# DeltaNet and SwiGLU on one core: eighteen sums of weight words from GpSimd to VectorE, other useless products at the start, and a new order of issue

## The chip, the cores and the metric

The kernel runs on one core of one Trainium2 chip. The metric is the device time of one execution in microseconds. Its engines run beside each other, each its own queue in order: TensorE (PE, with its weight loads PEld), VectorE (DVE), ScalarE (ACT), GpSimd (POOL), and SyncE (SP), which issues nearly all DMAs.

## The reference

Four batches, eight heads, 768 steps and heads of 48 go through the DeltaNet recurrence. The result, as 3072 tokens of 384 values, goes through an RMS norm and a SwiGLU feed-forward of width 1536. All of it is float32.

```python
k_n = k / (np.linalg.norm(k, axis=-1, keepdims=True) + 1e-06)
for t in range(S):
    y[:, :, t] = einsum('bhd,bhde->bhe', q[:, :, t], state)
    v_old = einsum('bhde,bhd->bhe', state, k_n[:, :, t])
    state = state + beta_t * einsum('bhd,bhe->bhde', k_n[:, :, t], v[:, :, t] - v_old)
x  = y.transpose(0, 2, 1, 3).reshape(B * S, H * D)          # 3072 x 384
xn = x / sqrt(mean(x * x, -1) + 1e-06) * rms_g
g  = xn @ w_gate                                           # 384 x 1536
out = (silu(g) * (xn @ w_val)) @ w_out                     # 1536 x 384
```

## The kernel before

**Chunks.** The 768 steps are cut into 12 chunks of 64. Within a chunk the recurrence is a triangular system, which is solved by an inverse; only the 48x48 states pass from one chunk to the next. Chunks 0 and 1 have their inverse made on VectorE by blocks of 16, in one long chain (L711 to L873: scaled scores, a transpose, small eliminations in 128x8 to 128x256 pieces, then products with the off-diagonal blocks on TensorE at L833 and L866). From chunk 2 on the chunk's matrices are shuffled by DMA and solved in another form (L935 to L1016).

**One chunk's recurrence.** K is loaded and squared (L604, ScalarE), summed over a head (L605, VectorE) and raised to a power for its norm (L609 and L628, GpSimd); K and Q are turned by TensorE (L560) and copied out (L570, L572); the scores are K times K (L692) and Q times K (L583). V is scaled by beta (L1145), multiplied with the inverse (L1202), with K's part (L1226; its operand comes from L833 by the copies L842 and L844), each copied out to `u` (L1216, L1218, L1238, L1240, L1245, L1247), and with the masked scores `pt` (L650) into the output (L1180). The products with the state stand at L1103, the state's update at L1273, its copy out at L1399. Then come the sums of squares (L1298, L1316), the root on GpSimd (L1323), the scaling (L1334, L1338), a turn (L1361), and the feed-forward.

**Feed-forward.** For chunks 0 and 1 it is the plain one: the up products for gate and value (L1433), the gating (L1441 on ScalarE, L1442 on VectorE), the down products (L1415). From chunk 2 on the products are saved in part by sums of weight blocks, made once on VectorE (L1491, L1493) and used at L1528 and L1585.

**Weights.** `weights()` brings the three weight matrices in as 18 pieces. The words of a piece are split by ScalarE into a high part (L500) and a low part (L501), the high part is shifted by three bits on VectorE (L495), and the sum of the two (L498) is written to `w_in` or `wo_sb`, from where TensorE reads it. A piece is 128 x 768 words; the buffers `xf`, `kk`, `more` and `tmp` hold the parts.

**What sets the order.** Each operation is recorded by `P.add(engine, duration, function, priority, ...)` and nothing is issued at that time. `Plan.run` issues all of them in the order that the string `ORDER` gives: two characters for the number of one operation, so that an operation added or taken away shifts the numbers of those behind it. The order is thus written out for every engine and queue, SyncE's DMAs too. The durations in `P.add` serve only to place useless products: where the plan leaves TensorE idle for more than 0.8 us, before `UNTIL` = 110 us of the plan, a list of them is put in front of the next TensorE operation. Such a product multiplies the identity with itself (L1707; widths of 128, 256 or 512 columns) into a bank that is not in use. A zero in the list stands for a tiny product of 32x1 (L1705). The first list, at time 0, is written by hand:

```python
    if a == 0.0:
        return [4, 4] + [0] * 13
```

One product in float32 is two records or more in the trace: the list's two products of 512 columns are four records, its thirteen tiny ones 26.

Of the kernel before, what the change touches and what calls it, by code (L numbers as in the profile page):

```python
# [12 lines left out]
ALU = mybir.AluOpType  # L13
# [3 lines left out]
C = 64  # L17
W = 32
# [26 lines left out]
    ",=*S*R,>,?,r+g(k,@,A*T,B+j*U,C,s,D(p*V,E,t,F(q,G(r,H,I*W(v,u*^(x(s*O*X.X*Y(u*_(t*`*Z(w*|,J.Y*[.Z*d*a,v,K*f*M*e*b*~,L"
    "*g.[*j,M+$*k*h*c*],N*t+%+k,O*l*i.]+#*u*p*N+h,P*v*P+(*w,Q*}+,,R+&*m.^,S*q+l*n+',T+-*x*o,W+)+.+m._+**y*r+4,U+/*z,X+2*s"
    "+n,V+5*{+6+p,x/F+3+:+7+++8.`+o,c+0+>+q,e+9,b.a+;,^+s+?+r,f,y):,[.c,d.b+B,g.n,'.g+F+C+<.d+@.e+t+=+x,(,`+u+N+G.f+A,a+H"
    "+1+v/E+J+D+y,h+w+K,_+z+{.5,Z+I,i+L,]+E,Y+|,j+O,{.h+P+M.i,l+},n,z,k,m.6.o.7+T+~+Q+V/M,#.;,$+U/L,%,&.8+W&.,~.j-$/G.k-&"
    ".l.m.p+R.q/H.r.s.t.<.u+Z.v+S/I.9.w-'.x/J+X+[.y-%&/.=+].z.:-#-(.{.>.|/K+Y-*1/.?-).@+_.W-+10.}11-0+`+^.~.B,|-,.A-1+b-2"
    "+a.C--12-8/#-..D-6.E-3.F/$-N-7-4-/-:-9/%-<13-5/&-P-=.G-R-Q/'-;-F.V-S->14-G-V/(.H-H/),}-B-I-Z-O-C/*-T15-[-D/+-J-?.I-U"  # L50
    "-c-E/,-W-]-d//-K-@-a/.-L16/-0h1y-M-A17-b-^.J0j-g-_18-X-e19-h-i/N-f/=1D-q/:-`-j1<-m-r1:-}1;-s-n-k1=-Y/<-o-l-t/2-p-u/9"
    "-y/8.#0i/1-v/;.K1>-w1?/>-x.L-{/3/O-z/7/?.M.)/4.N/@1E/6.O.'/R.P.Q/C/P/A/5-~/B/0-|.R.S.%.T.(/D.*1x/Q1@.-.$1A1B.&1C1F1G"
    "0n1H..1I1J.01K0k/T0o1L.U.+1M1z1N1O/V1{/U/X1|1P/W0l/Z.,/Y1}1Q0p.10m1R1S/].2/[1T.40q2$1~1U/_/^3b/c0r0s/e/`0t3c/d0%0u./"
    "/f/S0v/i1V.30'1W0x0w/k1X3e/j/m0y/g1Y/a3d/o1Z/n/l1[0)/b1]/p/u3f/h1./y1^0(2#/v0*/q0z/z/}1b/{/|012%0&3g0-/w1_020+1a/r1`"
    "2&/s0,/x091-3h0.030{/~0:2)070#040/1k0?0$1h2(081p0;/t3w4N3i0=1c0<0|053>1o061l0@3j1g2'0A1m0>0C1n3k3@1f3l0G0}0D3o1q0E0H"
    "3p0K001r3n0F3x3m0B0S3?0I4O0J1e0L1i1s0~1j0M0U1d0N1t3r0Q1v1#0O3q1$1w0[2+1%0Y0T1u1&0P0V0R3D1'1(1)1*3A0]0W1+3B1,3F3s0Z3C"
# [12 lines left out]
    ";U;X;Y9i8>;Z9d;[;]8?<1;^;_<2;`9k;a<39m;b9l8@;&8C;c9j8B9g9n;d9e9o;e8D8A;#8E9q<48F9p=t9u9r9w9v9{;f=u<6:7;%=v;g9}9x;'9~"
    ";h9|=w9y9h;i:%<5;(:#;):&;*:';j:$=x:/;+9z;k9s:+;,:0:9:,:1:;;-:(:::2:3=y:)9t:8;l:?:-;.;m:<:=;/:.;n:C:*;o:>:f=z:4;p9f:D"  # L70
    ";@:E:@;0;t:K:F;q:I={:G:5:A:M:L:6;1<7=|:J;r:N;s:H:O:B=};?=~:U:P;2:Q:b>$:V>#:Y<%:R:W>&:^:X:S;y:Z=P>%:T:[<=:_<8:];3:`:c"
    ">-<$:h:a:d:g=Q>(:e<:<#:l;v;4;u>':n;5;};6:j>.;{:i:o<&;7:m;w;8;~;9:r;::k<><9;z;;=R;<:p;x;=;><;:s>);|>*:t>+<?>,>/<A>0>1"
    ">2>3<'>4=S<(>5<B>6<)>7<C<-:q<*>8<G<,=T>9<@:v<+<D>:>;=V:w><:y<E<<=X=W=U:u<K>=:x=Y<F<H>><I<Q<L<M<R=r<S<N<W<J<T=Z<O=[<U"
    "<X=^<j>?=]<b<V>@=_<^<c=`<Y>A<d=a<l<P=b<e<Z<k<n<_<m<p>B<o<`=s<r<[<a<q<f=c<s<v>a>C<x<g<w<h<|<y=d<~<i>D<}=$<]=#<z=&<t=%"
    "=(=e>E='=,>c>F=0=-=<<u=.=)=f<{>G=*=/>J=1=4=8>I=2>d>H=3=g>b?x=+=h=5=i?{=j=9===6=>?|=7=k>S=:>f>W=l=B=m>V=n>O=;=?>P=o=D"
    ">U=@=C>X=E>R>N=p>K=q=H=A>g=I=K>Y>M=F>T>Z>h>L=J>Q>i=G?y>k>j>[>l>m>`?}=L>^>n>_>]?z>s=M=N>o>t=O>u>e>p?~>q>{@$@#>v>y@%>z"
    ">w>|?#@&?5?$?7@'>r@(>}?->~@)?9?.@*?)?/?:?0?%?*?6?A@+?&@,?;>x@-?'?8?(?1?+?<?=?,?B?C?2?>?I?3@.?D?G?4?J?K?H?M?L@/?S?N?O"
    "?T?W?P@0?[?Q?X?E?d?R?Y?]?U???Z?^?V?@@1?f?F?e?_?b?`?a?j?c?l@2?h?m@3@4?k?g@5?p@6?i@7@8@9@:@;?n@<?q?s?r@=?o@?@>?t@@@A@C"
    "@B?u@E@D?v@I?w@F@h@J@O@K@P@Q@L@U@R@M@j@G@V@S@N@`@T@k@l@a@p@H@b@m@c@[@i@t@]@n@u@d@o@W@q@e@v@X@f@|@Y@w@z@g@x@Z@^@y@~@_"
    "@{A$A#@}A*A%A&A+A.A,A'A2A-A(A/@rA:A)A0A1A3@sA<A4A;A5A6A7A?A8A=A9ALADAKA>ABAAAFACAEA@AMAGAHAJAIANAPAO"  # L80
# [176 lines left out]
def kernel(  # L257
# [17 lines left out]
    nc = tc.nc  # L275

    B, H, S, D = q.shape
# [17 lines left out]
    ident = sbt("ident", [128, 128])  # L295
# [98 lines left out]
    P = Plan()  # L394
# [72 lines left out]
    def weights(first, last):  # L467
# [14 lines left out]
        for n, (dst, src, keys) in list(enumerate(todo))[first:last]:  # L482
# [14 lines left out]
            def added(dst=dst.bitcast(U32), top=tiled(top), rest=tiled(rest)):  # L497
                nc.gpsimd.tensor_tensor(out=dst, in0=top, in1=rest, op=ALU.add)  # L498
# [5 lines left out]
            P.add("POOL", 1.87, added, pr, r=cvk + cak, w=done)  # L504
# [131 lines left out]
    qkeys = [("q2", 0, 0), ("q2", 0, 1), "q2p"]  # L636

# [239 lines left out]
    def prep(c):  # L877
# [824 lines left out]
    def filler(n, warm):  # L1702
        for w_ in n:
            if not w_:
                nc.tensor.matmul(warm[0:32, 0:1], ident[:, 0:32], ident[:, 0:1])  # L1705
                continue
            nc.tensor.matmul(  # L1707
                warm[:, 0 : 128 * w_].rearrange("p (w n) -> p w n", n=128), ident, ident[:, None, :].to_broadcast([128, w_, 128])
            )
# [33 lines left out]
```

## Time and profile before

| | us |
|---|---|
| runs | 660.82, 663.33, 663.36 |
| median | 663.33 |
| profiled execution | 663.93 |
| its span in the trace | 662.2 |
| TensorE busy | 650.7 (98%) |
| VectorE busy | 538.9 (81%) |
| ScalarE busy | 300.1 (45%) |
| GpSimd busy | 172.1 (26%) |

The profile comes from one execution, which is not one of the three timed runs. Times in the timeline count from the span's start. In rows of the timeline the first number is the start and the second the duration, then follow the engine, the line, the operation with its output and input and its shape; in brackets stands how long the engine idled before it and who ended that. In rows that group instructions the total and the mean in ns stand behind the bar. In rows by stretch each engine's busy time stands with its count of instructions in brackets, then TensorE's granted clock (1.00 is full), the share of the DMA engines and GB/s.

### The profile page before, as it was taken

To read this page: it belongs to the slowest core of one execution; us is meant where nothing else is said; L and a number is where in the kernel's file an instruction comes from. 1 tells how busy PE (TensorE), PEld (TensorE's weight loads), DVE (VectorE), ACT (ScalarE), POOL (GpSimd) and SP (SyncE) were. 2 spreads that over 40 slices of the span, in tenths; PEclk is the share of its full clock that TensorE was granted. 3 is DMA by queue.
4 is the path that set the end of the run, shared out by engine and by line. 5 is a ranking of instruction groups with operands and counts; after the bars stand their busy time and mean duration, and the time that the engine had idled before them with its cause. 6 is when DMAs were issued, how large, how long until landed. Compare 5 with 4: busy or idle time off the path is not lost.

```text
span 662.2 us, 23310 instructions
## 1 busy us (share of the span) xinstructions
PE 650.7 (98%) x9976; PEld 597.9 (90%) x9976; DVE 538.9 (81%) x1125; ACT 300.1 (45%) x712; POOL 172.1 (26%) x219
## 2 busy tenths in 40 slices
PE   9999999999999999899999999999999999999997
PEld 5587777877799999899999999999999999999997
DVE  5969779999799788898898898898899888457363
ACT  4776653235247245345344445444444354243240
POOL 4364790131600610520511330520511300000000
PEclk9998999999999999999999999999999999999999
DMA  9897754736295577276356476566167324211101
GB/s 221 224 229 190 245 138 89 122 54 103 75 135 99 129 146 117 35 151 111 71 103 120 90 142 102 87 128 95 41 122 122 71 49 82 37 38 25 25 2 24
DMA packets 270583, 69.36 MB, mean 105 GB/s; under 512 B 257488, under 2 KB 262736, under 8 KB 270160
## 3 DMA queue, kind: packets, MB, share of 16 engines
q1 hardware_dynamic: 269360, 67.63, 51.4%
q8 instruction: 78, 1.28, 0.8%
q10 hardware_dynamic: 1120, 0.25, 0.2%
q14 instruction: 25, 0.20, 0.1%
HBM read 49.76 MB, written 22.02 MB: 108 GB/s over the span
## 4 chain that ended last, share of the span: by engine, by line
PE 92%; DVE 4%; ACT 2%; issue 1%; POOL 0%; DVEq 0%; POOLq 0%; ACTq 0%
PE bank L1528 41%; PE bank L1585 20%; PE bank L1433 8%; PE bank L1415 5%; PE bank L1103 3%; PE bank L583 3%; PE bank L1707 2%; PE bank L1180 2%; PE bank L1166 2%; PE bank L1273 1%; PE bank L560 1%; PE bank L1045 1%; PE bank L1065 1%; PE bank L833 1%; PE bank L866 0%
## 5 line engine op out<-in xcount | busy, mean ns | idle before, releaser
L1528 PE MATMUL bank<-xf,w_in 128*128 128x128 f32 x1440 | 180.5, 276 | 0.0
L1528 PEld LDWEIGHTS bank<-xf,w_in 128*128 128x128 f32 x1440 | 170.2, 192 | 2.1 <-DVE acc L990 0.2
L1538 DVE TENSOR_TENSOR tmp<-tmp,bank 128x512 f32<-128x512 f32 x180 | 120.0, 682 | 42.1 <-PE bank L1528 36.4
L1528 PE MATMUL bank<-xf,more 128*128 128x128 f32 x960 | 122.0, 276 | 0.0
L1528 PEld LDWEIGHTS bank<-xf,more 128*128 128x128 f32 x960 | 114.6, 192 | 0.8
L1540 ACT COPY tmp<-bank 128x512 f32<-128x512 f32 x120 | 68.1, 586 | 95.9 <-PE bank L1528 69.5
L1544 ACT ACTIVATE tmp<-tmp 128x256 f32<-128x256 f32 x120 | 47.6, 415 | 72.3 <-DVE tmp L1538 72.1
L996 DVE TENSOR_REDUCE acc<-acc 128x30 f32<-128x90 f32 (+4 forms) x150 | 70.9, 473 | 5.2
L1585 PE MATMUL bank<-wo_sb,hf 128*128 128x192 f32 x360 | 64.0, 329 | 0.0
L935 POOL TENSOR_TENSOR at<-at,beta_b 128x256 f32<-128x256 f32 (+3 forms) x32 | 22.0, 718 | 158.1 <-DMA at<-dkk 139.1
L990 DVE TENSOR_TENSOR acc<-acc,at 128x60 f32<-128x60 f32 (+4 forms) x150 | 53.0, 353 | 10.5 <-POOL at L970 7.4
L1585 PEld LDWEIGHTS bank<-wo_sb,hf 128*128 128x128 f32 x360 | 58.1, 190 | 1.2 <-issue 0.4
L1545 DVE TENSOR_TENSOR hf<-tmp 128x256 f32<-128x256 f32 x120 | 47.6, 416 | 4.8 <-ACT tmp L1544 3.9
L628 POOL TENSOR_TENSOR knrm<-ksum,half 128x16 f32<-128x16 f32 x11 | 32.8, 2982 | 41.8 <-DVE ksum L607 40.2
L1415 PE MATMUL bank<-wo_sb,hf 128*128 128x384 f32 x96 | 35.6, 504 | 0.6 <-issue 0.6
L1433 PE MATMUL bank<-xp,w_in 128*128 128x256 f32 x144 | 35.2, 390 | 0.9 <-DVE hf L1442 0.9
L1016 POOL COPY acc<-acc 128x128 f32<-128x128 f32 x40 | 17.1, 459 | 69.1 <-DVE acc L996 67.7
L1433 PE MATMUL bank<-xf,w_in 128*128 128x256 f32 x144 | 33.1, 383 | 0.0
L1433 PEld LDWEIGHTS bank<-xp,w_in 128*128 128x128 f32 x144 | 27.0, 192 | 6.3 <-DVE hf L1442 1.3
L1385 DVE TENSOR_TENSOR xf<-xf 128x256 f32<-128x256 f32 (+1 forms) x70 | 29.1, 446 | 2.3 <-ACT xf L1355 1.8
L1433 PEld LDWEIGHTS bank<-xf,w_in 128*128 128x128 f32 x144 | 26.9, 190 | 4.3
L1322 POOL TENSOR_SCALAR ms<-ms 128x2 f32<-128x2 f32 x11 | 3.6, 331 | 93.6 <-ACT bank L1310 93.6
(221 smaller groups left out, 1024.5 us busy)
## 6 DMA issues: line engine op xcount, KB each, us to landing
at<-dkk SPq DMA_DIRECT2D x20, 256.0 KB, 4.3
vt<-in_v_dram SPq DMA_DIRECT2D x24, 192.0 KB, 4.3
k<-in_k_dram SPq DMA_DIRECT2D x23, 192.0 KB, 4.3
out_dram<-tmp SPq DMA_DIRECT2D x46, 96.0 KB, 2.2
dks<-k SPq DMA_DIRECT2D x14, 256.0 KB, 2.8
kt<-dks SPq DMA_DIRECT2D x28, 128.0 KB, 3.2
more<-in_moe_w_gate_dram SPq DMA_DIRECT2D x4, 768.0 KB, 7.0
more<-in_moe_w_out_dram SPq DMA_DIRECT2D x4, 768.0 KB
```

Source lines behind the costliest of these rows:

```text
L628: P.add("POOL", 2.95, lambda: nc.gpsimd.tensor_tensor(out=knrm[i2], in0=ksum[i2], in1=half, op=ALU.pow), pn, r=[("ksum", i2), "half"], w=[ ...
L990: nc.vector.tensor_tensor(out=acc[:, 1:3, 0:n, j + 2 : W].rearrange("p a i t -> p i a t"), in0=acc[:, old, 0:n, j : j + 2, None].to_broadc ...
L996: nc.vector.tensor_reduce(out=acc[:, new, 0:n, j + 2 : W], in_=acc[:, lo : lo + 3, 0:n, j + 2 : W].rearrange("p a i t -> p i t a"), axis=A ...
L1385: P.add("DVE", V(128 * n), lambda dst=dst, a=a, b_=b_, op=op: nc.vector.tensor_tensor(out=dst, in0=a, in1=b_, op=op), pxv, r=[("xp", 0), ( ...
L1415: nc.tensor.matmul(po[p].t[:, 0:DM], hf[:, spot(f), 128 * p : 128 * p + 128], wo_sb[:, spot(f)], start=(f == f0), stop=(f == f1 - 1), skip ...
L1433: nc.tensor.matmul(ps.t[:, TOK * side : TOK * side + TOK], w_in[:, side, h_, 3 * t + i_, n : n + 128], x_[:, 2 * t : 2 * t + 2].rearrange( ...
L1528: nc.tensor.matmul(g.t[:, 128 * z : 128 * z + 128], fac[:, side, 128 * f : 128 * f + 128], xf[:, xs], start=(begin and z == 0), stop=False ...
L1538: P.add("DVE", V(512), lambda t=t, g=g: nc.vector.tensor_tensor(out=t, in0=t, in1=g.t, op=ALU.add), -1, r=[g], w=[tk], last=g)
L1540: P.add("ACT", A(512), lambda t=t, g=g: nc.scalar.copy(t, g.t), -1, r=[g], w=[tk], last=g)
L1544: P.add("ACT", A(256), lambda t=t: nc.scalar.activation(out=t[:, 0:256], in_=t[:, 0:256], func=ACTF.Silu), -1, w=[tk])
L1545: P.add("DVE", V(256), lambda t=t, f0=f0, p=p: nc.vector.tensor_tensor(out=hf[:, spot(f0) : spot(f0) + 2, 128 * p : 128 * p + 128], in0=t[ ...
L1585: nc.tensor.matmul(g.t[:, 0:192], a_[:, f], b_[:, f], start=(begin and f == 0), stop=(f == 5), skip_group_check=True)
```

## The change

1. In `weights()` the sum of the high and low words (L498) is issued on VectorE instead of GpSimd. In the built program that is one instruction over half words, 1536 in each partition, for most pieces written as 3 rows of 512; the other operands and the order of the four steps of a piece are as before.
2. The first list of useless products becomes two of 512 columns and one of 256 columns, in the place of two of 512 and thirteen of 32x1.
3. A new function `ahead` records twelve of the tiny products as an operation of the plan, recorded in `prep()` for chunk 0 ahead of the turn of Q. In the built order they stand behind the 64 records of the scores and the turn of the betas (L660).
4. `ORDER` is another string: all operations of all engines and queues have a new order, and the places and widths of the later useless products follow from it. In sum the useless products have 10,624 columns for 11,520. In the built program VectorE has 8 of the 18 sums ahead of the last small elimination of chunk 1 (L762 before), three of them between chunk 1's scaled scores and that step; the other ten stand ahead of the first step on chunk 2's matrices (L935 before). In TensorE's order fifteen up products follow the state's update of chunk 0 where twelve did, and the state's product L1103 comes ahead of chunk 1's L583 and no longer behind it.

Lines from L638 on are 9 or 10 higher in the changed kernel (L1145 is L1155, L1433 is L1443).

```diff
@@ ORDER = ( ... )   every line of the string is replaced
@@ def fillers(a, b):
     if a == 0.0:
-        return [4, 4] + [0] * 13
+        return [4, 4, 2]
@@ weights()
             def added(dst=dst.bitcast(U32), top=tiled(top), rest=tiled(rest)):
-                nc.gpsimd.tensor_tensor(out=dst, in0=top, in1=rest, op=ALU.add)
+                nc.vector.tensor_tensor(out=dst, in0=top, in1=rest, op=ALU.add)
...
-            P.add("POOL", 1.87, added, pr, r=cvk + cak, w=done)
+            P.add("DVE", 0.97, added, pr, r=cvk + cak, w=done)
@@ ahead of qpart()
+    def ahead(n, pr):
+
+        def tiny():
+            for _ in range(n):
+                nc.tensor.matmul(banks[0][0:32, 0:1], ident[:, 0:32], ident[:, 0:1])
+
+        P.add("PE", 0.07 * n, tiny, pr, r=["ident"], size=4 * n)
+        P.ops[-1].ready = 10.0
@@ prep()
         if c == 0:
+            ahead(12, 14.0)
             P.urgent = 300.0
             qpart(0)
@@ def filler(n, warm):
         for w_ in n:
-            if not w_:
-                nc.tensor.matmul(warm[0:32, 0:1], ident[:, 0:32], ident[:, 0:1])
-                continue
             nc.tensor.matmul(
```

More of the change, by code (lines that the diff above doesn't have):

```diff
@@ new lines @@
+    "#|#g#~#}#h#r#1$##t#2$$#?$l#E$%$&#]$)$($'$*$>$+#J%L$-$,#D$/$.#N#K$0#L#@%O$3#O$q$4#P%z$5$?#F$@#Q$m$7$A$6%M$B#G&$$n$o#="
+    "%P$C#;#i%N#l#j$r#9#A$E#k$D$G$F$h$H$b$t$I$v$p$J$K$j%Q#8$T$L#B$M$U%y$i$V$O$W$N$1%$%[$X$Y$P%U$Z$Q$S$8$[$]$R$^%R%V&7$9${"
+    "%W%S$k$d&C&8%T$s%X$c$_%)$u&9&;%Y%Z&:$e&<%](%$f&?%{#6&=%^$a&>&@%_%`$2$`%a$w&E%|'$$}%b$x&&%c&A%3&F'%%%&%%}%d#5&D&G&B%~"
+    "'&&'%f&I&(%&&H$|%'&J%e%h%8$~&K%#%=%.%g%5%(&{&L&)$y%+%k&M&#%*&~&N'B%l%m%j%B%9&O%4%,%i'C&S&|%-'E$z%:%n%;%>&T&}%p%/%o%<"
+    "'F%s%@%?&U%u'Q'?&*%q%6(&%t&X%r'#'D%0%A%v%G%1#7&P%2%w%x'G&Q%C&R'''H'I&Y&V'K&W('%7'J&Z'L'+%D'M&_#:((&[%H#<()&`'(')'*&]"
@@ new lines @@
+    "%J(*','N&a%I&+'<'R'-&b&d'.'@(z'0({&e'/'A%E(+'1'O&i%K'>'2)_&j&f&g&,&1'4%F(-&k&n'3&2'=(,)b'P*B&^'S)`&c'T'U)a&5)c'V'8&3"
+    "'W&o'9'5'X':'6';)d'7'Y'Z)<)f'[)e&h&p)i'])j&m&l&4'^&6&r)h'_)g&s&q'`(6'a'b(:'c(;'d'e(7(.'f)l)k&t)+(8(<'g(9(=(/)>&x)8)?"
+    "'j'h(>(|'k&u'i(}(?),)-(D(@(0(~(E's(1'u)='r(B(C(A(F'v)#)n'q)m(I'y)o'x't(G)@(J'n)p'l'p(N)q)r(K'w)s'm'z'o)t*A(O)u'{*H(L"
+    ")v'|&z(P(S(2)w($*I(#'})x'~(H&y(4)y)B)z(M(Q){(3*C(X)|)A)D(Y)C*D(T*E)})~)E*F(U(Z*#*$(R(V*%,q)$(^*&(5([*G&w)](c*')F)G(_"
+    ",*)H*(**(d*)).)^*+,-)/,+,p)9(W,,(`,.)0+d*7(e(a)I*0)%,/*5)&)J*1(h)'*9,0(f*3,1)1*4(i)L+f,4,<*J*8(m)K*,)2,3):,5(n,2*2)3"
@@ new lines @@
+    ")Q*.)M+e*6)R(])4)N*/)O)S)((j*-)P*:)T)5,7*K)6,6*;,=,x)U)V*<)W&-*L(b*?)X(o(k*=,w)Y*@+g)7*>)Z*P))+j)**N(g)[+k,8&v(p,r*M"
+    ",9*R,:+h,;,>(l*S,?,s,@,A,B*T,C(q,D*U,t,E&.,F(r,u,G*V,H(s,I,J*X(w*W(t*Z+i,v(u*Y*_.Y(v*[(x*a*`*e,K.Z(y*},L*f.[+#*b*g,M"
+    "*c*k.],N*h*]*i+l*d*l+$*m*^*j,O*u*n*q.^*v*Q+%,P*w+m,Q+&*x*r*~+),R*s._,S+'/G+n,T*t*O+-+o*o+(,U*y+.+/+*.`*z+5,X+0*{,V+3"
+    "*p+6,W*|,y+q+7,Y+4+;/F+8.a+1+9+p+++?+r+:,b.b,),f+<+t,e+s,z+@,c+=.c,g+,);+G.d,h+A.f+C+>.e+H+y.g+D+u+z+O.h+2+v+w,],(+x"
+    "+E,d,{+{+I,_+B+|.6,[+}+F+~,|,i.j+Q+J,Z+M,j,a.7+P.o,`,#+K,^.p,k.i+L-#+U,$,l+W,},o,m.8,n&/,%.9+N+X.<,&.:+R,'+S.k.l-$.m"
@@ new lines @@
+    "/H.n.q,~-%.r+T.s.;/N.t-'.u+V/I.>.v+[.=.w/J.x.y/K.?.z.{+]+Y.|-&+_&0.}+^-+/L.W10-)+Z.@.A+`-*.~-(11.B12/#--1z+a.C-,+c-1"
+    "+b.D-.-3-213.E-7.X.F/M/$-9-8.G/%-/-O-:/&-=14-4-Q/'-5-;->-S-0-<.H/(-G-T-6-?15-H-C/)-I-R.I-J-[/*-P-D-W/+-@-U-E16-]/,-K"
+    "-V-d-X/--L-Y-^//-F-M.J-Z-b17/00i/.-N-_1y-c18/O-e-f-A/91:-B.K19-h/:-g1=-j-`-i/1-n-a/8-z/=/P-k/>-o1>-l-r1E1<-{1;/Q-v1F"
+    "/<-s/4-~-w/5-t-p/S-m-x-u/;-q.L/?1?.$1@-y.M0j/7.N-|.#/6.O.*/2/@.(/3.P/T0k.Q-}.R.S.&2$.T.).U.+.%1A/A/R1B..1C/D1D/E1G/C"
+    "/B1H.'1I1J0o1K1L0l1M0q0p1N.,1{1O0m.V./0n1P.1/W.01|/U0r1}/X1Q1R1~/Y.-1S.2/Z1T/V1U/[.32#.5/^0s/].43c1//`/_0&0t1V3d0v/d"
@@ new lines @@
+    "3e0u/a/f4O/e0w/j1W/l/g/k3f1X0x0(2%/b/m1Y0*0y/c0z/p1Z0+/n1[3g/q/r/o1]/h/z2&1^/v0{/i/{1_020)3h/|2'/}1b/w0.0'0|/s/x1`0,"
+    "031./~/y3i0-0:0/1c0#041a0;00080$1l051m0@0%1i093j0}0</t061o0>/u1k010=1f2)3k1q0A1p0?3?1e3l2(1n3m0D0~3@0B073n0H0E3o3p1r"
+    "0F0I3q0L0P4P0J1s0C0T3x1d0M1h1#0N0O1t1$3r0G1%0K3B1&1j1v1g1'1w1(1u0V3s1)1x3A3y1*0R0U1+0Q4W0Z0S0]2*4V1,3E1-0[0^0X0W3t3F"
+    "3u4Q3v3w3z0a3{0Y3|3}3~4R4#2.4$0b4S0d4%202/4&4T224'210_4(4)244*264U0`2X69230e254+6:0c272:6;0f4,0h2@0g2;2<4-6<2B2A4.2,"
+    "2F2C2=2Z2G2>3C2D4/6=2P402E3G2-2H2?282Q2]412R3D2L2I2[293H6>2S2^422+2Y432_443I2M2a453J2N2`2T6?3L3K2O2e462b3M482U2g492f"
@@ new lines @@
+    "2V2k3N2h3O2m6@2J3P2o472W2K7&6A2l4X2n4>2p2q4B6B2w6C3Q2r6D2s2x6N6G2{6E2t2i6F2c3#3a6O4C2j2|4Y3R2y2u3$4F2}3+4E2~3%2d4G2v"
+    "6I2z3'3S3-3(3,6H3&3)4D3*3b314[4Z333T3/4=347'3.4@6J4H4<306K5r4_6L3U4I6M326P4;4J6Q4A5t3V6R354?5s6S6T4N4:4K6U3W3X6V4L7."
+    "3Y4M373Z6W6X366Y5x3[3]5u3^6Z3;7(383_5z3`6[4a7)3<5v3=4c7*5y4b4`6]5w4e3:4d7+4]6^5{4f6_4g6`4m4h4^4i7,5|9X8l5}5/3>4n5~39"
+    "4o4j6#6a8m4u6$7-4p4s9Y6b516c4t4w6%6d8o4v4y6&6e4x536'4z4k4q8n4{6f4l6g5'684r54678p5#6h525(5;6(5$5)575*6k7/506j5+5%4|55"
+    "8q5,4}6l705<6)5&568H6i715=588r5C5>5A4~5?8I6*5-5D5E5.596s5B5I5:6v5F5@6r5G8s6x6z5M5H6y6p8t5N6+5J6n5Q8v5Y6w8u6u5U729%5R"
```

66 lines of the change are left out of this document (18 added, 48 removed).

## The prediction

> **What bounds the kernel now.** I read the page's shares and its chain first, then the windows by stage, the useless products by themselves, the chain of waits over the first 60 us, and last the timeline and the groups around the edited steps.
>
> ```profile
> PE 650.7 (98%) x9976; PEld 597.9 (90%) x9976; DVE 538.9 (81%) x1125; ACT 300.1 (45%) x712; POOL 172.1 (26%) x219
> PE 92%; DVE 4%; ACT 2%; issue 1%; POOL 0%; DVEq 0%; POOLq 0%; ACTq 0%
> ```
> ```profile
> 60.00:100.00 40.00, 39.08 (x696) 30.21 (x696) 29.89 (x56) 25.39 (x49) 31.24 (x21) 0.99 0.72 200
> 100.00:662.00 562.00, 555.85 (x8337) 526.98 (x8335) 464.35 (x958) 234.77 (x574) 112.13 (x172) 1.00 0.47 86
> ```
> ```profile
> 0.00:44.20 44.20, 23.74 (x68) 12.30 (x68) 1.00 0.92 211
> 44.20:60.00 15.80, 0.18 (x1) 0.00 (x0) 0.92 0.72 223
> ```
>
> The columns of the windows are the stretch, the busy time of PE, weight load, VectorE, ScalarE and GpSimd, then the granted clock. TensorE is busy 98% and 92% of the last chain is its own. But the last two rows, which hold the useless products alone, show that 23.74 us of its busy time before 44.20 us is filler. So the program has two halves. From about 60 us TensorE has a full queue (39.08 of 40, then 555.85 of 562 us, and a few per cent of records can be missing), and its work there is the same in both kernels: nothing can be gained, only lost. Before 60 us TensorE waits for VectorE and ScalarE, and the gain or loss of this change is made there.
>
> ```profile
> 1.41 3.78 PE bank L1707 x4
> 5.19 1.48 PE bank L1705 x26
> 6.67 1.90 PE bank L560 x8
> ```
> ```profile
> 5.79 0.84 ACT L604 ACTIVATE r<-k 128x768 f32<-128x768 f32 x1 [2.50 <-DMA k<-in_k_dram]
> ```
>
> **The start.** ScalarE begins on K at 5.79 us, when the load has landed. TensorE turns K only at 6.67, because the thirteen tiny products are still running (1.48 us). In their place stands one product half as wide as those before: two of the four records at 3.78/4 = 0.95 us, halved, are 0.95 us. So K's turn starts at 5.19 + 0.95 = 6.14, **0.5 us earlier**, and the steps behind it that have only this to wait for move with it. The twelve tiny products come back behind the scores and the betas' turn, at 1.48 x 12/13 = 1.4 us at the same speed, or less at the full clock; they delay q's turns by that, and a filler follows those in the new order too. That filler is the cover, since ScalarE copies q's turns only behind two sets of scaled scores: I charge nothing, and 1.4 us at most if the copies come up against them.
>
> **The sums.** Eighteen sums leave GpSimd and join VectorE's in-order queue.
>
> ```profile
> L498 POOL TENSOR_TENSOR w_in<-xf,tmp x6: 1812/1827/2017, 27.5 to 82.7; 128x768 uint32<-128x768 uint32 x6
> ```
> ```profile
> L495 DVE TENSOR_SCALAR xf<-xf 128x768 uint32<-128x768 uint32 x9 | 8.2, 909 | 1.2 <-ACT xf L500 1.0
> L495 DVE TENSOR_SCALAR kk<-kk 128x768 uint32<-128x768 uint32 x4 | 2.2, 553 | 1.2 <-ACT kk L500 1.2
> L1493 DVE TENSOR_TENSOR more<-more,w_in 128x512 f32<-128x512 f32 x1 | 0.7, 691 | 0.0
> L935 DVE TENSOR_TENSOR at<-at,beta_b 128x1024 f32<-128x1024 f32 x1 | 1.2, 1217 | 0.0
> ```
> ```profile
> 28.83 1.12 DVE L495 TENSOR_SCALAR xf<-xf 128x768 uint32<-128x768 uint32 x1
> 29.68 1.95 POOL L498 TENSOR_TENSOR w_in<-more 128x768 uint32<-128x768 uint32 x1
> 29.88 2.56 DVE L1145 TENSOR_TENSOR vt<-vt,rb 128x768 f32<-128x768 f32 x1
> 45.61 0.61 DVE L711 SCALAR_TENSOR_TENSOR acc<-m1bd,side,acc 128x128 f32<-128x128 f32 x2 [1.32 <-ACT acc L706]
> 47.67 2.17 DVE L711 SCALAR_TENSOR_TENSOR acc<-m1bd,side,acc 128x128 f32<-128x128 f32 x2
> 91.85 2.30 DVE L1493 TENSOR_TENSOR more<-w_in 128x512 f32<-128x512 f32 x1
> ```
>
> The trace has no such sum on VectorE. Two floating-point rows of the same form give a slope: (1.217 - 0.691)/512 = 1.03 ns an element, so 768 words at one word a cycle are 0.69 + 256 x 1.03 = **0.95 us**. The new program holds the sum as 1536 half words; one half word a cycle would be 1.217 + 512 x 1.03 = **1.74 us**, the other end. I take 0.95, because the shift of the same words (0.553 us for 768) runs no slower than a word a cycle. Eighteen are 17.1 us (31.3 at the other end).
>
> [...]
>
> VectorE gets something back. While GpSimd adds, VectorE's own work is stretched: V's scaling takes 2.56 us and ends 0.8 us after the sum beside it; by the slope it needs 0.95. The surplus is 1.61 there, (0.909 - 0.553) x 9 = 3.2 in the shifts of xf, 2.17 - 0.61 = 1.56 at the second pair of L711, and 2.30 - 0.69 = 1.61 at the last row against the undisturbed form of its line: together **8.0 us**. Net VectorE takes on 17.1 - 8.0 = 9.1 us, 23.3 at the other end. GpSimd loses 18 x 1.83 = 33 us, worth nothing by itself (0% of the chain).
>
> ```profile
> 24.12 1.48 POOL L885 TENSOR_TENSOR k<-k,krec 128x768 f32<-128x768 f32 x1 [7.13 <-DVE krec L632]
> 52.65 3.04 POOL L628 TENSOR_TENSOR knrm<-ksum,half 128x16 f32<-128x16 f32 x1 [2.53 <-DVE ksum L607]
> 53.07 0.29 DVE L754 TENSOR_TENSOR at<-at 128x128 f32<-128x128 f32 x1
> ```
>
> GpSimd keeps K's scaling (1.48) and the power steps. A power step stretches nothing: the two-input step of VectorE inside it takes 0.29 us for 128 elements. K's scaling has no such neighbour in the trace; if it held up a sum for its whole length three times, that were 4.4 us of VectorE's time, and I leave it in the range of the rival that fills VectorE.
>
> [...]
>
> **What becomes of it before 44 us.**
>
> ```profile
> 26.24 0.90 ACT L501 ACTIVATE tmp<-more 128x768 uint32<-128x768 uint32 x1
> 26.96 1.14 PE L866 MATMUL bank<-kk,x2bd 64*64 64x32 f32 x64
> 28.16 0.75 DVE L873 TENSOR_TENSOR mt<-mt,bank 128x256 f32<-128x256 f32 x2 [0.32 <-PE bank L866]
> 32.84 0.68 DVE L650 TENSOR_TENSOR pt<-bank,mask_p 128x512 f32<-128x512 f32 x1
> 35.01 0.48 DVE L844 TENSOR_SCALAR kk<-bank,side 128x256 f32<-128x256 f32 x1 [0.18 <-PE bank L833]
> 35.48 1.55 PE L1226 MATMUL bank<-u,kk 64*32 64x48 f32 x64
> 36.99 0.36 DVE L1240 COPY u<-bank 128x192 f32<-128x192 f32 x1 [1.50 <-PE bank L1226]
> 37.38 0.56 DVE L1247 COPY u<-bank 64x384 f32<-64x384 f32 x1
> 40.03 0.16 DVE L1316 SCALAR_TENSOR_TENSOR ms<-ms 128x1 f32<-128x1 f32 x1 [1.62 <-ACT yn L1298]
> 44.21 1.03 PE L1433 MATMUL bank<-xp,w_in 128*128 128x256 f32 x4
> ```
>
> L866 ends at 28.1 now, at 27.6 then. Ahead of its reader VectorE has a sum that can start once ScalarE has made both halves (about 27.1) and ends at 28.05. Two products of L873 (0.75 together) and a shift (0.55) bring V's scaling to 29.35 and, at 0.95, to 30.3 instead of 32.44: 2.1 earlier. Behind it stand a shift, a sum, K's copy (0.48) and U's first copy (taken as the 0.56 of the like one): L1226 can start near 32.9 instead of 35.48. Then a sum, three shifts and masks (0.55 + 2 x 0.68 + 0.55) and the two copies of U (0.36 + 0.56) end at 37.2, where they ended at 37.94: **0.75 earlier**, so three sums cost 2.85 of what was won. Up to the first product of the feed-forward (44.21) two more sums stand around L1316, where VectorE idled 1.62 us: covered, with at most 0.3 lost. Another reading of the same stretch: the new list holds 10,624 columns of filler for 11,520, so 23.74 x 896/11,520 = 1.85 us less stands in TensorE's queue. Between 0.75 and 1.85 I take **1.3 us**.
>
> **44 to 60 us.**
>
> ```profile
> 50.85 0.91 DVE L605 TENSOR_REDUCE ksum<-r 128x16 f32<-128x768 f32 x1
> 55.50 1.51 PE L1103 MATMUL bank<-state,qt 48*64 48x48 f32 x64 [0.99 <-ACT state L1399]
> 56.94 2.35 PE L1433 MATMUL bank<-xp,w_in 128*128 128x256 f32 x6
> 84.51 1.56 PE L1433 MATMUL bank<-xp,w_in 128*128 128x256 f32 x6
> ```
> ```profile
> 50.00:60.00 10.00, 8.96 (x152) 7.24 (x151) 9.55 (x24) 7.34 (x14) 5.50 (x4) 0.88 0.52 155
> 60.00:70.00 10.00, 10.00 (x157) 7.21 (x156) 8.68 (x21) 6.45 (x13) 4.56 (x3) 0.95 1.03 292
> ```
>
> TensorE idles 0.99 us for the state, which ScalarE copies late because its queue stands behind VectorE's chain; the clock then falls (0.88, 0.95 in the two windows), and the same six products take 2.35 instead of 1.56 us. 0.12 of the one window's 10 us and 0.05 of the other's are 1.7 us of TensorE's time. Idle and fall are worth 2.7. In the new order three sums (2.85) stand in that chain, less 1.56 of lost stretch and the 0.91 of a reduction that now stands behind it: 0.4 later. But three more up products stand ahead of the state's reader, and chunk 1's scores behind it. I take half of the 2.7: **1.3 us**, ends 0 and 2.7.
>
> **60 to 100 us.** Ten sums (9.5) come, and of the stretch 3.2 - 0.57 + 1.61 = 4.2 us go (all but the shift at 28.83 lies here): 29.9 + 9.5 - 4.2 = 35.2 us of VectorE's 40. It fits. Three sums wait for a TensorE group of 1.5 us that shares a weight tile; behind them queue a shift, chunk 1's transposes and the feed-forward's gating, whose readers on TensorE are a group or more away. I charge 0, ends 0 and 3.
>
> Sum: -1.3 - 1.3 = -2.6. The profiled execution took 663.93 (span 662.2 and 1.7 around it), 0.6 above the median of 663.33; on the median the forecast is **660.7**.
>
> **Rivals.** (1) *All waits go.* 1.85 before 44 us, 2.7 after it, and the 0.92 us that TensorE lacks between 60 and 100 (39.08 of 40): -5.5, 657.9, with a spread of 656.5 to 659.5. For it: VectorE's queue loses its stretched pieces just where TensorE waits for them. Against: ten sums go back into the same queue. (2) *VectorE becomes the bound.* At 1.74 us a sum the three before 37.2 cost 3 x 0.79 = 2.4 more, which turns 0.75 won into 1.6 lost; the three ahead of the state's copy another 2.4, less what the new order covers, say 1.2; and between 60 and 100 VectorE has 29.9 + 17.4 - 4.2 = 43.1 us for 40, 3.1 too many. 1.6 + 1.2 + 3.1 = +5.9: 669.2, or 666.1 where the queue on TensorE covers the last. It decides from 0.95 + 0.75/3 = 1.2 us a sum on. Against: the shift's row. (3) *The clock takes the gain.* The tiny products at 11 us come in a stretch of small products; a fall of the same size there would cost 1.7 us, in fillers that stand ahead of useful work, and turn the start's gain of 1.3 into 0.4 lost: 662.4. Against: the thirteen before did not keep the clock from rising.
>
> **The numbers.** Forecast (659.2 to 662.2) 0.43, rival 1 0.24, rival 2 0.23, rival 3 0.10. A measurement here tells 0.5%, 3.3 us, from no change: below 660.0 faster, above 666.6 slower. Faster: rival 1 and a third of the forecast, 0.24 + 0.14 = 0.38. Slower: most of rival 2, 0.19. Same: the rest, 0.43. Eight in ten lie from 656.8 to 667.0: a little of rival 1 and half of rival 2 stay out.
>
> **What would show it.** In the profile after: a VectorE sum near 0.95 us; V's scaling near 0.95 and ended at 30.3; L1202's counterpart at 30.4; the first up product near 42.9; no half clock in 50 to 70 us. A sum over 1.2 us, or TensorE idle behind VectorE beyond 60 us, makes the forecast wrong.

## The result, and the profile after

The changed kernel takes 657.25 us (median of 4 runs, 654.99 to 658.64); the kernel before takes 663.28 (4 runs, 660.82 to 663.36). The ratio is 0.9914, with a 95% interval of 0.9888 to 0.9940: 6.0 us or 0.9% faster. The forecast was 660.7 with a range of 656.8 to 667.0. The range holds the result; the likeliest case (659.2 to 662.2) does not, and the first rival (657.9) comes within 0.7 us of it. By the prediction's own bound (below 660.0) the change is faster, to which it gave 0.38.

The profiled execution of the changed kernel took 654.99 us, with a span of 653.2: at the lower end of its runs, while that of before (663.93) was above all four of its own. The two profiles are therefore 8.9 us apart where the medians are 6.0 apart. First the page's busy times, then windows (stretch, busy times of TensorE, weight load, VectorE, ScalarE and GpSimd, granted clock, DMA share, GB/s):

```profile
PE 645.3 (99%) x9976; PEld 595.5 (91%) x9976; DVE 540.7 (83%) x1143; ACT 300.2 (46%) x712; POOL 137.5 (21%) x201
```
```profile
50.00:60.00 10.00, 10.00 (x162) 7.97 (x161) 9.65 (x26) 8.66 (x17) 2.91 (x1) 1.00 0.63 159
60.00:70.00 10.00, 10.00 (x224) 7.95 (x223) 9.89 (x19) 7.50 (x11) 2.96 (x2) 1.00 0.97 340
```
```profile
60.00:100.00 40.00, 40.00 (x822) 32.74 (x822) 34.09 (x68) 25.56 (x51) 14.62 (x12) 1.00 0.66 188
```

VectorE's busy time rose by only 1.8 us (540.7 for 538.9). By the records the eighteen sums take 17.7 us, and the other lines of VectorE take 11.5 us less than before: the shifts of L495 3.2, L1493 1.9, L1385 1.7, V's scaling and L711 1.6 each (numbers of lines as before). (The rest of the difference is overlap of records, which the busy time counts once: added up, all records of VectorE are 596.9 us for 590.8.) The clock stays full from 50 to 70 us (1.00 in both windows, 0.88 and 0.95 before), and TensorE has no gap from 60 to 100. The timeline of the changed kernel:

```profile
5.90 1.06 PE L560 MATMUL bank<-ident,k 128*128 128x128 f32 x8 [0.52 <-DMA k<-in_k_dram]
25.42 0.96 DVE L498 CUSTOM_DVE_ANT_0 w_in<-xf,tmp 128x1536 uint16<-128x1536 uint16 x1
27.60 0.95 DVE L1155 TENSOR_TENSOR vt<-vt,rb 128x768 f32<-128x768 f32 x1
28.60 1.15 PE L1212 MATMUL bank<-vt,mt 64*64 64x48 f32 x64 [0.22 <-DVE vt L1155]
33.28 1.55 PE L1236 MATMUL bank<-u,kk 64*32 64x48 f32 x64
35.79 0.56 DVE L1257 COPY u<-bank 64x384 f32<-64x384 f32 x1 [0.28 <-ACT u L1255]
41.65 3.07 PE L1443 MATMUL bank<-xp,w_in 128*128 128x256 f32 x12
52.40 1.15 PE L1113 MATMUL bank<-state,qt 48*64 48x48 f32 x64
54.43 1.56 PE L1443 MATMUL bank<-xp,w_in 128*128 128x256 f32 x6
```

V's scaling takes 0.95 us and ends at 28.55 (2.56 and 32.44 before); the first up product starts at 41.65 (44.21); the state's product comes at 52.40 without a wait (55.50 with 0.99). Two of the groups of sums (minimum, median and maximum in ns):

```profile
L498 DVE CUSTOM_DVE_ANT_0 w_in<-xf,tmp x6: 945/954/959, 25.4 to 76.0; 128x1536 uint16<-128x1536 uint16 x6
L498 DVE CUSTOM_DVE_ANT_0 wo_sb<-xf,tmp x3: 952/974/1592, 48.7 to 91.8; 128x1536 uint16<-128x1536 uint16 x3
```

The last place is far down the program. Here is what TensorE waited for after 100 us, in the kernel before and in the changed one (total, times, longest). "issue" means that nothing in the profile released TensorE:

```profile
PE bank L1585 <- DVE xp L1577: 1.7, 1, 1.7
PE bank L1415 <- issue: 0.6, 1, 0.6
PE bank L1585 <- issue: 0.4, 1, 0.4
```
```profile
PE bank L1538 <- issue: 0.5, 1, 0.5
```

The order of before lets TensorE stand 1.66 us at 268 us for a sum of the gated values `hf` on VectorE (L1577); the new order does not. In all, 2.7 us of waits become 0.5.

### The profile page after: what moved, and what is told of

Same layout as the page of the kernel before. It is cut to its first block, busy times and chain, and to the rows that moved or that the text cites. A ratio compares the mean times of both kernels' runs of the same rounds, so it can differ in the third digit from the quotient of the medians.

```text
span 653.2 us, 23284 instructions
## 1 busy us (share of the span) xinstructions
PE 645.3 (99%) x9976; PEld 595.5 (91%) x9976; DVE 540.7 (83%) x1143; ACT 300.2 (46%) x712; POOL 137.5 (21%) x201
## 3 DMA queue, kind: packets, MB, share of 16 engines
q8 instruction: 78, 1.28, 0.8%
## 4 chain that ended last, share of the span: by engine, by line
PE 91%; SPq 3%; DMA 2%; DVE 2%; issue 1%; POOL 1%; ACT 0%; POOLq 0%; DVEq 0%; ACTq 0%
PE bank L1538 40%; PE bank L1595 20%; PE bank L1443 10%; PE bank L1425 5%; PE bank L583 3%; SPq L402 3%; PE bank L1113 3%; PE bank L1714 2%; PE bank L1190 2%; PE bank L1176 1%; PE bank L1283 1%; PE bank L1055 1%; PE bank L1075 1%; PE bank L560 1%; DMA at<-dkk 1%
## 5 line engine op out<-in xcount | busy, mean ns | idle before, releaser
L1548 DVE TENSOR_TENSOR tmp<-tmp,bank 128x512 f32<-128x512 f32 x180 | 119.6, 682 | 42.9 <-PE bank L1538 33.1
L1538 PE MATMUL bank<-xf,more 128*128 128x128 f32 x960 | 124.1, 276 | 0.0
L1595 PEld LDWEIGHTS bank<-wo_sb,hf 128*128 128x128 f32 x360 | 57.9, 190 | 1.2 <-issue 0.4
L1425 PE MATMUL bank<-wo_sb,hf 128*128 128x384 f32 x96 | 34.7, 493 | 0.0
L1443 PE MATMUL bank<-xp,w_in 128*128 128x256 f32 x144 | 34.1, 386 | 0.0
L1443 PE MATMUL bank<-xf,w_in 128*128 128x256 f32 x144 | 32.8, 382 | 0.0
L1443 PEld LDWEIGHTS bank<-xf,w_in 128*128 128x128 f32 x144 | 27.0, 190 | 4.8 <-issue 0.2
L1443 PEld LDWEIGHTS bank<-xp,w_in 128*128 128x128 f32 x144 | 26.5, 190 | 4.5 <-DVE xp L1376 0.3
L1425 PEld LDWEIGHTS bank<-wo_sb,hf 128*128 128x128 f32 x96 | 17.1, 190 | 8.4 <-issue 0.2
```

The source lines that it names most:

```text
L1425: nc.tensor.matmul(po[p].t[:, 0:DM], hf[:, spot(f), 128 * p : 128 * p + 128], wo_sb[:, spot(f)], start=(f == f0), stop=(f == f1 - 1), skip ...
L1443: nc.tensor.matmul(ps.t[:, TOK * side : TOK * side + TOK], w_in[:, side, h_, 3 * t + i_, n : n + 128], x_[:, 2 * t : 2 * t + 2].rearrange( ...
L1538: nc.tensor.matmul(g.t[:, 128 * z : 128 * z + 128], fac[:, side, 128 * f : 128 * f + 128], xf[:, xs], start=(begin and z == 0), stop=False ...
L1548: P.add("DVE", V(512), lambda t=t, g=g: nc.vector.tensor_tensor(out=t, in0=t, in1=g.t, op=ALU.add), -1, r=[g], w=[tk], last=g)
L1595: nc.tensor.matmul(g.t[:, 0:192], a_[:, f], b_[:, f], start=(begin and f == 0), stop=(f == 5), skip_group_check=True)
```

## The experiments

The theory to begin with: GpSimd's sums stretch VectorE's work before 60 us, and taking them off is the gain. The rivals: the order alone, the start alone. In runs 1 and 2 `P.add` keeps its engine and duration, so that the order and the useless products stay as they were (10,624 and 11,520 columns). The runs of the kernel before beside these give medians of 663.3 (first four runs), 662.5 (next four) and 663.1 (last four).

**1. The sums back on GpSimd, in the new order.**

```diff
# changed kernel
-nc.vector.tensor_tensor(out=dst, in0=top, in1=rest, op=ALU.add)
+nc.gpsimd.tensor_tensor(out=dst, in0=top, in1=rest, op=ALU.add)
```

> The changed kernel with its eighteen sums issued on GpSimd again, in the changed order. Theory (the sums beside VectorE's work stretch it, and taking them off GpSimd is the gain): VectorE's V scaling takes over 2 us again, the first up product starts 1.5 to 3 us later than 41.65, and the time is 661 to 664 us. Rival (the new order and the new start are the gain, the engine of the sums is not): under 658.5 us.

Measured: 660.95 us (12 runs, 658.47 to 665.43), ratio to before 0.9968 (0.9946 to 0.9990). The changed kernel on the same chip (run 4) took 656.46, so 4.5 us are given back (3.8 by the two ratios, whose intervals do not meet): about what the theory gave, but not where it said.

```profile
27.60 0.95 DVE L1155 TENSOR_TENSOR vt<-vt,rb 128x768 f32<-128x768 f32 x1
27.83 2.41 POOL L498 TENSOR_TENSOR w_in<-kk,tmp 128x768 uint32<-128x768 uint32 x1 [0.57 <-DVE kk L495]
```
```profile
60.00:100.00 40.00, 38.21 (x703) 30.48 (x703) 30.39 (x50) 24.34 (x47) 32.22 (x23) 1.00 0.67 191
```
```profile
PE bank L875 <- DVE x2bd L833: 1.2, 1, 1.2
PE bank L560 <- POOL k L894: 0.4, 1, 0.4
```

V's scaling keeps its 0.95 us: in the new order it starts first, and GpSimd's sum takes 2.41 instead of 1.8. The first up product comes at 42.42, only 0.77 later. The larger loss is behind it: from 60 to 100 us TensorE lacks 1.79 us (the windows above, then its waits there), for chunk 1's transposes on VectorE and for K's scaling, which stands in GpSimd's queue among the sums. So the new order cures the stretch of V's scaling even with the sums on GpSimd, and on top of that order the sums' move pays most after 60 us, where the prediction had counted nothing.

**2. The sums alone on VectorE, in the order of before.** The edit is the other way round, in the kernel before.

> The kernel before with only the eighteen sums issued on VectorE, at the same places of the order. Theory (the stretch is what costs, but eighteen sums in places that were chosen for GpSimd stand in the way of VectorE's chain): 661 to 665 us, about the time before. Rival (the sums alone bring the gain, whatever the order): 657 to 659 us. Rival 2 of the prediction (VectorE becomes the bound): above 666 us.

Measured: 662.35 us (12 runs), ratio 0.9991 (0.9971 to 1.0011): no difference that can be told. V's scaling falls to 0.95 us here too, and starts at 27.94, yet the first up product comes at 44.93. The wait at L1585 is there (1.6 us). At the places of the old order the move of the sums is worth next to nothing, and with the new order and start about 4 us; these without the move are worth 2 (run 1). The whole is more than the sum of its parts.

**3. The start of before, in the new order.**

```diff
# changed kernel
-        return [4, 4, 2]
+        return [4, 4] + [0] * 13          # and the tiny products back in filler()
-            for _ in range(n):            # in ahead()
+            for _ in range(0):
```

> The changed kernel with the first list of useless products of before (two wide and thirteen tiny) and no tiny products behind the scores; its order is unchanged. Theory (the start is worth the 0.5 us by which K's turn comes earlier, and up to 1 more where the clock rises earlier): 657.7 to 659 us, K's turn at 6.6 us instead of 5.90. Rival (the start decides when the clock rises, and with it a window of 3.4 us at half speed): 659 to 661 us and the turns of K at 1.97 us again. Rival (nothing waits for K's turn): 657.2 us.

Measured: 661.87 us (12 runs, 656.91 to 666.65), ratio to before 0.9975 (0.9946 to 1.0004). That is 5.4 more than run 4, above all that was expected, though K's turn came at 6.35 us and took 1.09. Up to the product with V, at 28.9 us for 28.7 in run 4, the profiled execution is 0.2 us behind. The loss follows (the two largest of TensorE's waits over the whole run):

```profile
PE bank L1717 <- issue: 3.1, 1, 3.1
PE bank L842 <- issue: 2.2, 2, 1.5
```

TensorE stands 3.1 us at 31 us and waits for nothing that the profile shows; the clock then falls (a mean of 0.65 from 32 to 36 us and of 0.92 from 36 to 40). The edit also changed what the plan puts in: 11,392 columns of wide filler for 10,624, 1.6 us at the rate of before (23.92 us for 11,520). So this run is not the start alone.

**4. The changed kernel again.** No edit.

> The changed kernel as it is, on the chip and in the rounds of the other three, to have its spread. Both theories: 657.2 us within 2; if the early clock of the first profile (full from 4.6 us on) was chance, this profile shows the turns of K cold and the time nearer to 658; if it comes from the start, they take 1.1 us again.

Measured: 656.46 us (7 runs, 655.16 to 661.08). The profile has K's turns at 1.07 us again, but so have runs 2 and 3 with the start of before (1.06 and 1.09): in all twelve profiles of these runs chunk 0's scores start between 7.9 and 8.8 us. The profile before has 10.25 and slow turns of K (1.97 us). Since run 2 with the same start has 8.10, the start of before does not bring this by itself; it was most likely one late execution, but the kernel before was profiled only once. (Run 11, the changed kernel, has its turns at 1.91 us and the scores at 8.77.)

**5 and 6. The start alone, and start and sums without the order.** Kernel before, with `[4, 4, 2]` for the first list; run 6 also with the sums on VectorE.

> The kernel before with only its first list of useless products changed (two of 512 and one of 256 columns, none of the tiny ones anywhere); order and sums as before. Theory (K's turn starts 0.1 to 0.5 us earlier and later waits swallow it): 662.3 to 663.3 us. Rival (the start was worth 5 us in the changed kernel and is worth it here): 658 to 659 us.

> The kernel before with the changed first list and with the sums on VectorE, in the order of before: all of the change but the new order and the tiny products behind the scores. Theory (the order is what turns the sums off GpSimd into time, and the order of before waits 1.7 us for VectorE at about 268 us, which the new order does not): 661 to 662.5 us, with that wait of L1585 in its trace. Rival (sums and start are the gain, the order does not matter): 657 to 658 us.

Measured: 665.73 us (6 runs), ratio 1.0050 (1.0034 to 1.0067), and 666.29 (6 runs), 1.0052 (1.0033 to 1.0071). Both are slower than before, which neither theory nor rival had (the wait of L1585 is in run 6's trace, with 1.2 us). The products of L1707 alone, up to 60 us, in before, run 5 and run 6:

```profile
0.00:60.00 60.00, 23.92 (x68) 12.30 (x68) 0.98 0.87 214
```
```profile
0.00:60.00 60.00, 29.21 (x80) 14.48 (x80) 1.00 0.84 206
```
```profile
0.00:60.00 60.00, 28.92 (x80) 14.49 (x80) 1.00 0.83 206
```

The edit by itself adds 256 wide columns and takes thirteen tiny products away. But the plan's times shifted with it, and in all the plan put in 14,848 columns for 11,520. TensorE spends 5.3 and 5.0 us more on them, and the first up product starts at 48.3 and 48.6 us. In this kernel a change of the first list is not a change of the first list alone, so that the start by itself was not measured.

**7. No tiny products behind the scores.**

```diff
# changed kernel, in ahead()
-            for _ in range(n):
+            for _ in range(0):
```

> The changed kernel without the twelve tiny products behind the scores; the planned order is the same. Theory (they stand where TensorE would idle, and nothing waits for them): 656.5 us within 1. Rival (they keep the clock up over the stretch of small products at 10 us): a fall of the clock in the first 20 us and 658 to 659 us.

Measured: 654.98 us (4 runs, 654.86 to 655.33), ratio 0.9883 (0.9869 to 0.9898). The columns of filler stay 10,624. No fall of the clock (a mean of 1.00 from 0 to 60, from 60 to 100 and from 100 to 653 us). The time is below the theory's range and below the changed kernel's 656.46 (on another chip; run 12 compares them on one), and all its runs lie together.

**8 to 10. What is the 3.1 us stretch?** The traces show a DMA queue of the kind "instruction", q8, with 78 packets of 16,384 bytes (1.28 MB in the profile before and in the one after). That these are blocks of TensorE's instructions is the author's reading of what follows; no record says it. From the packets of that queue, with the records of TensorE (products and weight loads) that had begun when the third block started:

```
profile                   2nd block  3rd block  records  TensorE then idle ("issue")
changed, first              23.63      27.29      712     0.5
changed, run 4              23.77      27.24      704     0.9
run 3 (start of before)     25.68      31.10      954     3.1
run 1 (sums on GpSimd)      23.61      28.97      876     1.2
run 7 (no tiny)             23.73      30.99      927     1.2
run 8 (five cut short)      24.91      30.89      954     3.1
run 9 (run 3, one halved)   25.50      29.02      704     none there
run 10 (changed, one h.)    23.65      28.79      700     none
changed, run 11             26.11      31.35      954     3.3
run 12 (run 7 again)        23.69      29.91      909     none there
```

In the three with the stretch TensorE had begun the same number of records, 954, when the block came: it had come to the same place of its program, one product into the fillers behind V's product.

The traces say more than this table. The fourteen profiles of this case hold 33 idle stretches of TensorE that are put down to "issue". Every one begins when 699, 954 (or 953) or 1209 records have begun, or further whole steps of about 254.5 behind these (within 6 records), and ends 1.2 to 1.9 us after the end of one packet of that queue: at 699 the second block, at 954 the third, at 1209 the fourth. The queue brings 78 blocks for 19,952 records, about 256 each. So the stretches stand at fixed places of the count, and each ends shortly behind its packet. That TensorE has no further instruction there until the block has come is the author's reading of both. The kernel's own plan counts in the same way: `PACKET` and `fetch()` in `Plan.times` let TensorE wait for a block at 444.2 records and every 254.45 records from there, which gives 698.7, 953.1 and 1207.6.

Three runs tried whether the third block is late behind the loads of weights. In run 8 five pieces of run 3's kernel are cut short, in run 9 half of one piece is left out, in run 10 the same half in the changed kernel. In run 8 four of the five pieces still load 512 of 768 KB, since they have three parts of which two are kept, and the fifth, loaded by half, is issued only at 34.7 us; so this run took away less than its text says.

```diff
# run 9 on run 3's kernel, run 10 on the changed one
# run 8 on run 3's kernel: n in (2, 3, 4, 5, 6), keeps parts - parts // 2, zeroes the rest on GpSimd
+            if n == 7:
+                rdst, src = rdst[:, 0:1], src[:, 0:1]
             dma(rdst, src, 2 + 2 * n, w=[("raw", i)], ...)
```

> The changed kernel with the start of before, as the third run, but five of the early weight pieces are loaded by half and the rest of them is set to zero on GpSimd (the output is that of other weights). In the third run TensorE idled 3.1 us at 31 us with nothing in the trace that it waited for, 4 us after a block of its own instructions should have been fetched, while the DMA engines were full of weights. Theory (the block was late behind the weights): that idle stretch is under 0.5 us here, the block starts at 27 to 29 us and not at 31, and the time is 655 to 658 us. Rival (the start of before loses the time by itself): the stretch stays and the time is 660 to 663 us.

> The changed kernel with the start of before, as the third run, but of the weight piece whose load is issued at 26.6 us (the first of w_out in the buffer more) only half is loaded (the output is that of other weights). In the third run and in the one with five earlier pieces halved TensorE's third block of instructions starts only at 31 us, 4 to 5 us after that load was issued, though the DMA engines were nearly idle at 24 to 28 us in the latter. Theory (the block stands behind this one load): it starts by 29 us, the idle stretch of 3.1 us falls under 1 us, and the time is 657 to 659 us. Rival (the block is asked for late, whatever is loaded): it starts at 31 us again, the stretch stays over 2.5 us, and the time is 661 to 663 us.

> The changed kernel with the same half of that one piece left out, as the control of the ninth run. Theory and rival: the block starts at 27 us as it did, and the time is that of the changed kernel within 1 us, 655.5 to 657.5; if the half load by itself were worth more, the ninth run would say nothing.

Measured: run 8 659.03 us (10 runs, 657.46 to 663.58; the profiled one took longest and has the stretch), run 9 659.58 (12 runs, 657.19 to 663.81), run 10 655.86 (4 runs, 655.05 to 656.33), with ratios of 0.9951 (0.9934 to 0.9968), 0.9946 (0.9921 to 0.9970) and 0.9887 (0.9866 to 0.9908). The medians of runs 8 and 9 are 2.8 and 2.3 us below run 3's 661.87, and that of run 10 is 2.4 below the 658.30 of the changed kernel on its chip; by the ratios these are 1.6, 1.9 and 2.3 us, and the intervals overlap. In run 9 the stretch is gone (1.1 us of such idle time stands at L844, at 73.5 us), as the theory had it, though the block starts at 29.02, the median misses its range and some runs stay above 661. But in the profiled executions of runs 9 and 10 the clock fell at 11 us (a mean of 0.66 from 10 to 15 us in both), so that all of this stood some 1.7 us later, the load too (issued at 28.0 us): the blocks at 29.02 and 28.79 came on time, at about 700 records. The changed kernel had it on time in two of three profiles with the whole load, so one execution shows little, and run 10 is no clean control. In run 8 the DMA engines were nearly idle at 26 us (a share of 0.22 from 26 to 28) and the block was late all the same. That the load issued at 26.6 us has a part in it is thus argued, not shown; what makes the block late stays open.

**11 and 12. The changed kernel and run 7's kernel, side by side.** No new edits.

> The changed kernel as it is, beside the next run on one chip. 656.5 us within 1.5.

> The changed kernel without the twelve tiny products behind the scores, again, beside the changed kernel on one chip. Theory (the products are not needed, and 655.0 us of the seventh run is real): 654.8 to 655.6 us, 1 to 2 us less than the changed kernel beside it, with the third block of instructions at about 31 us again and a wait of 1 us at L1236. Rival (chance between chips): both at 655 to 657 us, within 0.7 of each other.

Measured: 658.30 us (8 runs, 654.80 to 661.19; ratio to before 0.9922, 0.9892 to 0.9951) and 654.17 (4 runs, 653.95 to 654.73; ratio to before 0.9864, 0.9844 to 0.9884). Run 11's profile took 660.85, and it shows the stretch in the changed kernel itself:

```profile
28.41 1.07 PE L842 MATMUL bank<-mt,m1bd 64*64 64x32 f32 x60 [1.00 <-issue]
30.41 0.48 PE L1714 MATMUL bank<-ident 128*128 128x256 f32 x1
34.19 0.97 PE L1714 MATMUL bank<-ident 128*128 128x256 f32 x5 [3.29 <-issue]
46.80 3.07 PE L1443 MATMUL bank<-xp,w_in 128*128 128x256 f32 x12
```
```profile
34.00:40.00 6.00, 5.81 (x80) 4.50 (x80) 0.06 (x1) 1.40 (x3) 0.00 (x0) 0.72 0.87 212
```

The first up product is 5.15 us later than in the first profile (46.80 for 41.65), of the 5.9 us between the two executions: 4.3 of idle time (1.0 behind the second block, 3.3 behind the third, for 0.5 in the first profile), and a clock of 0.72 over the next six. The spread of the changed kernel, whose 19 runs lie from 654.8 to 661.2, goes with the clock of its runs: the nine with a mean granted clock of 0.999 or 1.000 took 654.80 to 656.99 us, the ten with 0.995 to 0.997 took 656.54 to 661.19. That a block was late in each of these ten is a guess: it was seen in the one of them that was profiled. Of run 7's kernel none of 8 runs is above 655.4, and all have a clock of 0.999 or 1.000, though its third block came at 30.99 and 29.91 us (run 12's was expected at 31 with a wait of 1). It has 48 records less ahead of that place, and comes there later: in run 7 TensorE has begun 953 records, and stands, at 32.63 us, for 30.5 to 30.9 in the three with the stretch, and waits 1.2 us instead of 3.1 to 3.3. In run 12 there is no such stretch behind the third block, and one of 0.3 us behind the fourth, at 37 us. On one chip it beats the changed kernel by 4.1 us.

## Why the prediction was right or wrong

- **The sum on VectorE, 0.95 us: right.** Measured 0.895 to 0.974 for all but one of the eighteen: 1536 half words take what the slope gives for 768 elements, not the 1.74 us that it gives for 1536, and rival 2 fell with that.
- **A sum beside GpSimd's work: one of eighteen was stretched.** It took 1.59 us:

```profile
66.89 1.49 POOL L1138 TENSOR_TENSOR r<-r,bt 128x384 f32<-128x384 f32 x1 [2.32 <-DVE r L1135]
67.60 1.59 DVE L498 CUSTOM_DVE_ANT_0 wo_sb<-xf,tmp 128x1536 uint16<-128x1536 uint16 x1
```

It ends 0.81 us after GpSimd's product, nearly the length of a whole sum, as if it had waited; one row does not show why. The neighbour is L1138, not the scaling of K that the prediction had feared. No run shows the 4.4 us that were left in the range for that: over the eighteen sums of this profile the stretch is 0.64 us. What VectorE gets back was sized too small: 11.5 us for 8.0.
- **The start: the size of K's turn right, its profile not typical.** K's turn came at 5.90 instead of 6.14, and it waited for the load, not for fillers. But the profile before was 2.3 us behind at the first scores (10.25 for 7.98), more than any other profile of this case, so that the base of the forecast was a late execution at this place.
- **Before 44 us: 1.3 forecast, 2.56 between the profiles.** V's scaling ended at 28.55, forecast 30.3; U's copies at 36.35, forecast 37.2; the first up product at 41.65, forecast 42.9. The term was too small by half. How much of it is that late start isn't shown: run 2 with its scores at 8.10 has its first up product only at 44.93. Run 2 shows that the sums alone win nothing by this point, and run 1 that the order and the start with GpSimd's sums win most of it (42.42).
- **44 to 60 us: 1.3 forecast, 3.0 measured.** The next product with the state (L1118, L1128 in the changed kernel) stands here, in before and in the changed kernel:

```profile
64.00 1.15 PE L1118 MATMUL bank<-state,kt 48*64 48x48 f32 x64
```
```profile
58.41 2.75 PE L1443 MATMUL bank<-xp,w_in 128*128 128x256 f32 x12
61.09 1.15 PE L1128 MATMUL bank<-state,kt 48*64 48x48 f32 x64
```

It is 2.91 us earlier, and by then the changed kernel has done 60 records of the up products where the kernel before had done 48, and all else the same. Twelve records are 2.7 us of work. So it is 5.6 us ahead, of which 2.56 had been won before 44. Both the wait (0.99) and the fall of the clock (1.7) are gone: the upper end, 2.7, and a little more. To take half of it was the mis-sized step here.
- **60 to 100 us: 0 forecast, 0.92 won; after 100: 0 forecast, 2.2 won.** This is the step that failed: "its work there is the same in both kernels: nothing can be gained". The busy time of TensorE hid that it stood 0.93 us for the gating (L1442) at 95 us and 1.66 us for L1577 at 268 us, which its waits show (the second stands in the section on the result). The new order, which was costed only where the trace was read, removed both. The other 0.5 us after 100 are in stretches of "issue" (1.0 before, 0.5 in the changed kernel).

```profile
95.46 2.86 PE L1433 MATMUL bank<-xp,w_in 128*128 128x256 f32 x12 [0.93 <-DVE hf L1442]
```

- **The sum.** 2.56 + 3.0 + 0.92 + 2.2 = 8.7 of the 8.9 us between the profiles, where 2.6 was forecast. Up to 100 us this is rival 1, "all waits go" (5.5, here 6.5); the 2.2 after that are in no case of the prediction. That the median came to lie in the range is in part luck: the profile before was above all its runs and the profile after at the lower end of its own, and 8.9 us off the median of before would have lain outside.
- **Rival 3, the clock at 11 us: it occurs, and costs less than was priced.** Run 10, whose start is that of the changed kernel, shows the fall at that place (the row below). Run 9 shows it too (0.66 in the same window), and has no tiny products there, so that the fall comes without them:

```profile
10.00:15.00 5.00, 5.00 (x38) 3.55 (x39) 4.65 (x18) 3.30 (x12) 2.23 (x2) 0.66 1.00 342
```

0.34 of 5 us are the 1.7 us that the rival had, but this execution took 656.16, 1.1 more than the fastest of its four: some of the loss seems to be taken up by the fillers behind it. The harm that goes with the tiny products in the traces is another: with their 48 records TensorE stands at 954 records at 30.9 us in run 11, for 3.3 us; without them, in run 7, it comes to 953 only at 32.63 and stands 1.2.

## What to carry to other kernels

Before saying that nothing can be gained in a stretch, list the waits of the bounding engine there: 98% busy left room for waits of 0.9 and 1.7 us. A change of fillers has three prices: what is moved, what the planner then adds, and when TensorE comes to the records at which it stood here (699, 954 and 1209). Compare a single profile with the spread of the runs before its start is taken for the rule.

## What the runs showed of the hardware

In these profiles TensorE stood for "issue" only at fixed places of its program. All 33 stretches in the fourteen profiles begin at 699 records or a whole number of steps of about 254.5 behind that, and end 1.2 to 1.9 us after a packet of 16,384 bytes has come on the queue q8. That TensorE has run out of instructions there is the author's reading. In run 11's profile of the changed kernel the second block starts at 26.11 us instead of 23.63 and the third at 31.35 instead of 27.29; TensorE stands 1.0 and 3.3 us, and then the mean granted clock is 0.72 from 34 to 40 us: 1.7 of 6 us, as much as 3.4 us at half. The two stretches are 4.3 us in this execution, where the first profile of the changed kernel has 0.5.
